# Stated load order and eight banks at the first MLP seam, and grad_out times gb made in the input-gradient loop

## The chip, the cores and the metric

One core of a Trainium2 chip runs the whole program. A core has five engines that run side by side and wait for each other through semaphores: TensorE (PE; its weight loads are shown as PEld), VectorE (DVE), ScalarE (ACT), GpSimd (POOL) and SyncE (SP). Here SP and POOL mainly issue DMA transfers, each from a list of its own that it works through from the top. The metric is the device time of one execution in microseconds (us); lower is better.

## The reference

A block with an adaptive layer norm, a spectral filter and an MLP, forward and backward, in bf16, with S = 2048 tokens, D = 1024 and F = 3584:

```python
mod = (silu(c) @ w_mod).reshape(1, 6, 1, -1)      # sa, ca, ga, sb, cb, gb
h = layernorm(x) * (1 + ca) + sa
x = x + ga * irfft2(rfft2(h) * (w_r + 1j * w_i))
h = layernorm(x) * (1 + cb) + sb
x = x + gb * (gelu(layernorm(h) @ w1 + b1) @ w2 + b2)
_out, _vjp = jax.vjp(f, x, w_r, w_i, w1, b1, w2, b2, c, w_mod)
return (_out, *_vjp(grad_out))
```

The outputs are the forward result and nine gradients. Three of the backward products matter here. The gradient of the MLP's input is gz @ w1^T, where gz (F x S) is the gradient before the gelu. The gradient of w2 is h^T @ (grad_out * gb). The gradient of row 5 of the modulation, gb, is the sum over the tokens of grad_out times the MLP's result.

## The kernel before

The tokens are worked in four blocks (b = 0 to 3) of 512, D in two halves (h) of 512, and F in seven groups (g) of 512. Buffers in on-chip memory are handed from one use to the next by tag: a tile that takes a tag over waits until the previous owner was read for the last time. PSUM has eight banks in three pools: ps_s with two, ps_d with two, ps_f with four. A scheduler orders the instructions of each engine and each DMA list when the kernel is built, by priority and by its own estimate of the time; `tc.issue_after(x)` keeps an instruction behind x in that order, and `ordered()` keeps the matmuls of the MLP in the order in which they are written.

**The MLP.** For each block and g, `z_block` (L781 to L817) makes the first product (pz, L795) and the gelu with its derivative, and stores hh and gz to DRAM. For each block and half, `bo_pass` (L822 to L860) makes the second product: a matmul with b2 (L827) opens four accumulators pbo, and then seven steps of 16 matmuls each (L836) read hh and one piece of w2. The pieces of w2 come through four buffers (w2sA, w2sC, w2sD, w2sB), 56 loads of 512 KB in all; each is issued by SP at L831, and the scheduler places it. At the end of a pass ScalarE copies pbo to otile (L845), VectorE makes the output from it, three stores write it to out_0 (one from SP, L154, and two from POOL, L159), and a later matmul pa (L855) sums the tokens of grad_out times the result, which VectorE adds into gacc. The plan at L872 to L878 interleaves z blocks and steps of bo_pass; block 3 has no z blocks beside it.

**The first MLP seam.** After the last pass come its pa, and pq (L903), which turns gacc into grad row 5 (`store_gmod`, L905: two casts at L177 and a store to d_gmod, L178), and ptr, which turns the gradient of b1 (L913). Then come the loads of the transposed w1 (L968 to L974): 28 DMA transposes of SP, four for each g, into tiles w1T that take over the tags of w1. The gradient loop reads gz from DRAM through eight slots (gzr, L1013).

**The input-gradient loop** (L1001 to L1054) runs for each block. TensorE makes pg, 2 halves x 7 g x 16 matmuls (L1020), in the four banks of ps_f, one half after the other. ScalarE copies pg to gn3 (L1025). VectorE and ScalarE take it backward through two layer norms: `ln_bwd` (L917 to L924) against n3u (loaded at L1005), the product with n2u into pru (L1032), again a scale (L1041) and `ln_bwd` against n2u, then the addition of grad_out (go4, which lies in got; loaded by `load_tok` at L1009, half of it by SP and half by two gathers of POOL, L130) at L1045. The sum is stored to d_gx1 (L1046). Its product with ga goes to n3u (L1048), is folded twice between n3u and pru (L1049) and lands in fbuf2 (L1050). Its product with d_A (au, L1047) is made at L1051. TensorE sums gn3 and pru over the tokens into acc3a (`sums3`, L1035), and au into acc3b (`sums3_ga`, L1053), which stands in the code after the block's work. Between these steps `early`, a ring of eight steps for grad row 5 (`gmod_ring`, L942 to L966), is advanced: each step is a product with a sum (L958), a scale (L960), a store to out_9 from POOL (L961) and the load of a later piece of w_mod by SP (L947); the ring starts when d_gmod has row 5 (L950).

**The seam to the gradient of w2.** After the loop, grad_out is loaded once more, a block at a time, with `load_tok`, into gB0 to gB3, which take over the tags of w1T tiles, and VectorE multiplies each by gb (L1059 to L1065). TensorE then makes gw2acc (L1114) from them and from transposed pieces of hh (hht, `hh_load` at L1139), and after 256 of these matmuls the backward spectral transform begins with pu (L470), which reads fbuf2.

Of the kernel before, what the change touches and what calls it, by code (L numbers as in the profile page):

```python
# [10 lines left out]
FP32 = mybir.dt.float32  # L11
BF16 = mybir.dt.bfloat16
# [5 lines left out]
P = 128  # L18
# [17 lines left out]
def kernel(  # L36
# [42 lines left out]
    def ps_f(name):  # L79
        return psum.tile([P, 512], FP32, tag="f", name=name, bufs=4)  # L80
# [38 lines left out]
    def chunk_rows(dt, i):  # L119
        return dt[4 * i * P:4 * (i + 1) * P, :].rearrange("(q p) d -> p q d", p=P)  # L120
# [4 lines left out]
    def load_tok(t4, src, i, eng=None):  # L125
        s3 = tok_flat(src)
        ins = (eng or nc.sync).dma_start(out=t4[:, 0:4:3, :],
                          in_=bass.AP(tensor=s3.tensor, offset=s3.offset + 128 * i * D, ap=[[D, P], [1024 * D, 2], [1, D]]))
        for q in range(2):
            nc.gpsimd.indirect_dma_start(out=t4[:, 1 + q, :], out_offset=None, in_=s3,  # L130
                                         in_offset=bass.IndirectOffsetOnAxis(ap=xidx[:, 2 * i + q:2 * i + q + 1], axis=0))
        return ins
# [687 lines left out]
    w2n = [0]  # L820

    def bo_pass(b, h):  # L822
        cs_ = slice(h * KH, (h + 1) * KH)
        pbs = [(ps_f if b < NB - 1 or h == 0 else (ps_s, ps_d)[k % 2])("pbo") for k in range(4)]
        for i in range(4):
            with ordered():
                last_pe[0] = nc.tensor.matmul(pbs[i][:], lhsT=ones_bf[0:1, :], rhs=b2_row[0:1, cs_], start=True, stop=False)  # L827
        for g in range(7):
            wp = w2p[w2n[0] % 4]
            w2n[0] += 1  # L830
            nc.sync.dma_start(out=wp, in_=w2_v[:, g * 4:(g + 1) * 4, cs_])  # L831
            hh = hh_slots[(b * 7 + g) % 11]
            for i in range(4):
                for k in range(4):
                    with ordered():
                        last_pe[0] = nc.tensor.matmul(pbs[i][:], lhsT=hh[:, k, i * P:(i + 1) * P], rhs=wp[:, k, :],  # L836
                                                      start=False, stop=(g == 6 and k == 3))
            if g < 6:
                yield
        bo, x1t, go = (otile[0][:, k] for k in range(3))  # L840
        nc.sync.dma_start(out=x1t, in_=chunk_rows(d_x1, b)[:, :, cs_])
        load_tok_half(go, grad_out, b, h)
        for i in range(4):
            with tc.high_priority():
                last_ev[0] = nc.scalar.copy(out=bo[:, i, :], in_=pbs[i][:])  # L845
        tt(go, go, bo, ALU.mult)
        tt(bo, bo, bcn(gb_row[:, cs_], 4), ALU.mult)
        tt(bo, bo, x1t, ALU.add)
        store_tok_half(out_0, bo, b, h)

        yield
        pa = (ps_d if b < NB - 1 else ps_f)("pa")
        for i in range(4):
            with ordered():
                last_pe[0] = nc.tensor.matmul(pa[32 * i:32 * (i + 1), :], lhsT=ones_bf[:, 0:32], rhs=go[:, i, :], start=True, stop=True)  # L855
# [24 lines left out]
    for kind, b, g in plan:  # L880
# [7 lines left out]
        else:  # L888
# [6 lines left out]
                bo_late.clear()  # L895
            if g == 13:
                next(boq[b], None)
    for late in bo_late:
        next(late, None)
    g5 = []  # L900
    for h in range(2):
        pq = (ps_s, ps_d)[h]("pq")
# [62 lines left out]
                load_w(n + 2)  # L965
            yield  # L966

    w1Ts = []  # L968
    for g in range(7):
        wtile = reg.tile([P, 4, D], BF16, name=f"w1T_{g}", tag=W1T[g])  # L970
        for k in range(4):
            fc = g * 4 + k
            nc.sync.dma_start_transpose(out=wtile[:, k, :], in_=B_w1[:, fc * P:(fc + 1) * P])
        w1Ts.append(wtile)  # L974
    gzr = [reg.tile([P, 2, 4, BW], BF16, name=f"gzr{k}", tag=f"t{k}") for k in range(4)]
    gn3s = [reg.tile([P, 4, D], BF16, name="gn3a", tag="uv0"), reg.tile([P, 4, D], BF16, name="gn3b", tag="wt")]
    n3u = reg.tile([P, 4, D], BF16, name="n3u", tag="uv1")
    n2u = reg.tile([P, 4, D], BF16, name="n2u", tag="uv2")
    pru = reg.tile([P, 4, D], BF16, name="pru", tag="uv3")[:]
# [3 lines left out]
    gzn = 0  # L983
# [14 lines left out]
    def sums3_ga(b, p4):  # L998
        halves_sum(acc3[1], p4, b == 0, b == 3)

    for b in range(NB):  # L1001
        gn3 = gn3s[b % 2]
        sums = small.tile([P, 2, 4], FP32, tag="sums")
        gzt = []
# [5 lines left out]
        for g in range(7):  # L1010
            sl = gzr[gzn % 8 // 2][:, gzn % 2]
            gzn += 1
            nc.sync.dma_start(out=sl, in_=d_gz_v[:, g * 4:(g + 1) * 4, b * BW:(b + 1) * BW])  # L1013
            gzt.append(sl)
        for h in range(2):
            pgs = [ps_f("pg") for _ in range(4)]
            for g in range(7):
                for i in range(4):
                    for k in range(4):
                        nc.tensor.matmul(pgs[i][:], lhsT=gzt[g][:, k, i * P:(i + 1) * P],  # L1020
                                         rhs=w1Ts[g][:, k, h * KH:(h + 1) * KH],
                                         start=(g == 0 and k == 0), stop=(g == 6 and k == 3))
            for i in range(4):
                with tc.high_priority():
                    nc.scalar.activation(out=gn3[:, i, h * KH:(h + 1) * KH], in_=pgs[i][:], func=ACT.Identity,  # L1025
                                         accum_out=sums[:, h, i:i + 1])
# [20 lines left out]
        nc.sync.dma_start(out=au[:], in_=chunk_rows(d_A, b))  # L1047
        tt(n3u[:], g2[:], bcn(ga_row, 4), ALU.mult)  # L1048
        fold_tok(n3u, ftmp)  # L1049
        fold2_in[b] = fold_d(fbuf2[:, b], n3u[:], ftmp)  # L1050
        tt(au[:], g2[:], au[:], ALU.mult)  # L1051
        if b < NB - 1:
            sums3_ga(b, au)  # L1053
            next(early, None)  # L1054


    hhp = reg.tile([P, 2, NT, P], BF16, name="hhsA", tag="px1")
    gBs = []
    for b in range(NB):  # L1059
        gb_t = reg.tile([P, 4, D], BF16, name=f"gB{b}", tag=PXT[2 + b])  # L1060
        gb_in = load_tok(gb_t, grad_out, b)
        with tc.high_priority():
# [218 lines left out]
```

## Time and profile before

| what | value |
|---|---|
| median of 3 runs | 1510.4 us (1502.69 to 1513.5) |
| the profiled execution | 1507.2 us, its span 1505.0 us |
| mean granted TensorE clock | 0.978 |
| TensorE, VectorE, ScalarE, GpSimd busy | 1408.0 (94%), 1068.8 (71%), 721.4 (48%), 371.6 us (25%) |
| moved by DMA | 324.27 MB, mean 215 GB/s |
| hardware queue (SP), software queue (POOL) | 51.3%, 22.5% of the 16 DMA engines' span |

The stages around the change, from the windows of the profile (the columns after the engine's name are its busy time and, in brackets, its instructions; then the granted clock, the DMA engines' busy share, and the rate):

```profile
core 0: us, PE busy (x) PEld busy (x) DVE busy (x) ACT busy (x) POOL busy (x), PEclk, DMA share, GB/s
...
720.00:740.00 20.00, 17.38 (x81) 7.64 (x82) 7.54 (x15) 0.00 (x0) 4.21 (x4) 1.00 1.08 366
...
760.00:780.00 20.00, 15.46 (x66) 6.37 (x67) 4.96 (x6) 6.56 (x8) 1.48 (x3) 0.93 0.55 187
...
880.00:940.00 60.00, 55.05 (x265) 24.42 (x268) 48.66 (x72) 23.07 (x34) 4.20 (x3) 1.00 0.45 158
...
990.00:1000.00 10.00, 0.84 (x3) 0.30 (x4) 2.29 (x1) 0.00 (x0) 2.47 (x1) 0.61 1.09 213
1000.00:1010.00 10.00, 6.18 (x17) 2.06 (x16) 6.16 (x8) 0.09 (x1) 0.00 (x0) 0.70 1.05 284
```

How to read a profile: a page gives each engine's busy time, then the chain of work that ended last, followed back from the end, with each engine's share of it. In a row of a timeline stand the start, the length, the engine, the line, the operation, what it writes and reads, how many instructions are merged in the row, and in brackets how long the engine sat idle before it and what ended that. Idle time of an engine costs something only if it delays the work that ends last.

### The profile page before, as it was taken

How to read it: one execution, taken by the hardware profiler on the slowest of the kernel's cores; microseconds unless marked ns; L12 is line 12 of the kernel's file. 1: busy time of each engine (PE TensorE's matmuls, PEld its weight loads, DVE VectorE, ACT ScalarE, POOL GpSimd, SP SyncE). 2: the span in 40 equal slices, each digit the busy share in tenths (PEclk: the TensorE clock that was granted, in tenths of full speed). 3: DMA queues.
4: the chain of work that ended last, by engine and by line, in shares of the span. 5: the costliest groups of instructions: out<-in, count | busy, mean ns of one | idle time of the engine just before them, and what ended most of it. 6: DMA issues, size and time to landing. Idle time of an engine off the chain costs nothing.

```text
span 1505.0 us, 18218 instructions
## 1 busy us (share of the span) xinstructions
PE 1408.0 (94%) x6703; PEld 655.0 (44%) x6835; DVE 1068.8 (71%) x1574; ACT 721.4 (48%) x960; POOL 371.6 (25%) x427
## 2 busy tenths in 40 slices
PE   5899989999999999999889999969999999899998
PEld 2434545444444444444334444424454444444443
DVE  5883777898799888877413877959067776997551
ACT  4765446757887755666111433313532344453211
POOL 5710631210112122212112001220124421222432
PEclk8999999999999999999999999989999999999999
DMA  9982664899687777899956246398379987675992
GB/s 336 265 223 67 156 212 137 264 245 338 225 252 230 233 243 231 247 279 262 344 195 221 76 180 224 107 214 211 98 188 241 248 221 222 175 198 149 275 294 92
DMA packets 358168, 324.27 MB, mean 215 GB/s; under 512 B 209191, under 2 KB 300861, under 8 KB 357824
## 3 DMA queue, kind: packets, MB, share of 16 engines
q1 hardware_dynamic: 324192, 207.71, 51.3%
q0 software_dynamic: 33888, 115.41, 22.5%
q8 instruction: 53, 0.87, 0.2%
q14 instruction: 35, 0.29, 0.1%
HBM read 164.15 MB, written 109.10 MB: 182 GB/s over the span
## 4 chain that ended last, share of the span: by engine, by line
PE 42%; DVE 19%; DMA 8%; issue 6%; ACT 5%; POOL 1%; SPq 0%; POOLq 0%; DVEq 0%; ACTq 0%
PE pbo L836 10%; PE pz L795 10%; PE gw2acc L1114 8%; PE gw1acc L1181 4%; PE pg L1020 4%; DVE ct L172 4%; DVE got L919 2%; PE pu L470 2%; PE pv L563 2%; ACT ct L460 1%; DVE gn3a L924 1%; DVE st L436 1%; DMA gB<-in_grad_out_dram 1%; DMA n3u<-d_n 1%; DMA w2sA<-in_B_w_dram 1%
## 5 line engine op out<-in xcount | busy, mean ns | idle before, releaser
L678 PE MATMUL pp<-gBoT,wt 128*128 128x512 bf16 x878 | 198.2, 383 | 4.9 <-DMA wt<-in_B_w_dram 2.0
L1020 PE MATMUL pg<-w1T,gzr 128*128 128x512 bf16 x876 | 195.2, 381 | 1.5 <-issue 0.7
L1181 PE MATMUL gw1acc<-gzh,n3n 128*128 128x512 bf16 x876 | 195.0, 381 | 1.1 <-issue 0.2
L678 PEld LDWEIGHTS <-wt 128*128 128x128 bf16 x896 | 88.0, 98 | 110.0 <-issue 6.1
L795 PEld LDWEIGHTS <-w 128*128 128x128 bf16 x896 | 87.5, 98 | 109.4 <-issue 6.0
L1020 PEld LDWEIGHTS <-gzr 128*128 128x128 bf16 x896 | 87.0, 98 | 108.5 <-issue 6.0
L1181 PEld LDWEIGHTS <-n3n 128*128 128x128 bf16 x896 | 87.6, 98 | 105.9 <-issue 2.4
L795 PE MATMUL pz<-n3Ta,w 128*128 128x512 bf16 x437 | 99.5, 383 | 2.9 <-ACT gt L798 2.1
L1114 PE MATMUL gw2acc<-gB,hhsA 128*128 128x512 bf16 x437 | 97.9, 379 | 1.0 <-DMA hhsA<-d_hh 0.4
L795 PE MATMUL pz<-n3Tb,w 128*128 128x512 bf16 x439 | 98.4, 379 | 0.5
L1119 ACT CAST gwo<-gw2acc 128x512 bf16<-128x512 f32 x54 | 30.5, 584 | 130.1 <-PE gw2acc L1114 84.1
L836 PEld LDWEIGHTS <-hhA 128*128 128x128 bf16 x608 | 58.9, 98 | 75.2 <-issue 5.1
L798 ACT ACTIVATE gt<-pz,b_col 128x512 bf16<-128x512 f32 x112 | 73.1, 683 | 35.6 <-PE pz L795 33.7
L1185 ACT CAST gwo<-gw1acc 128x512 bf16<-128x512 f32 x53 | 30.8, 582 | 115.1 <-PE gw1acc L1181 91.6
L804 ACT ACTIVATE gt<-gt 128x2048 bf16<-128x2048 bf16 x28 | 53.5, 1910 | 66.1 <-DVE gt L172 66.0
L172 DVE TENSOR_TENSOR gt<-gt,gt 128x2048 bf16<-128x2048 bf16 x56 | 68.5, 1223 | 21.6 <-ACT gt L806 20.9
L172 DVE TENSOR_TENSOR ct<-ct 128x2048 bf16<-128x2048 bf16 x64 | 75.9, 1221 | 10.3 <-ACT ct L631 9.0
L1114 PE MATMUL gw2acc<-gB,hht 128*128 128x512 bf16 x251 | 58.6, 393 | 14.4 <-DMA hht<-d_hh 10.3
L1114 PEld LDWEIGHTS <-hhsA 128*128 128x128 bf16 x448 | 43.6, 98 | 52.5 <-DMA hhsA<-d_hh 0.9
L800 ACT ACTIVATE gt<-gt 128x2048 bf16<-128x2048 bf16 x28 | 53.4, 1907 | 0.6
L806 ACT ACTIVATE gt<-gt 128x2048 bf16<-128x2048 bf16 x28 | 53.4, 1907 | 0.5
L1186 POOL DMA_DIRECT2D out_dram<-gwo x56 | 30.5, 546 | 84.5 <-ACT gwo L1185 74.3
(313 smaller groups left out, 2495.2 us busy)
## 6 DMA issues: line engine op xcount, KB each, us to landing
gzr<-d_gz SPq DMA_DIRECT2D x28, 512.0 KB, 6.4
wblk<-in_w_mod_dram SPq DMA_DIRECT2D x12, 1024.0 KB, 9.7
d_ph<-pho POOLq DMA_DIRECT2D x21, 512.0 KB, 5.6
out_dram<-otl POOLq DMA_DIRECT2D x40, 256.0 KB, 3.6
d_hh<-hhA POOLq DMA_DIRECT2D x19, 512.0 KB, 4.8
w2sD<-in_B_w_dram SPq DMA_DIRECT2D x14, 512.0 KB
hhC<-d_ph SPq DMA_DIRECT2D x14, 512.0 KB, 4.9
w2sA<-d_ph SPq DMA_DIRECT2D x14, 512.0 KB, 4.5
```

The source lines that it names most:

```text
L172: return nc.vector.tensor_tensor(out=out, in0=a, in1=b, op=op)
L678: last_pe[0] = nc.tensor.matmul(pp[:], lhsT=wt[:, fg % 2, cch, k * P:(k + 1) * P], rhs=gBoT[j][:, cch, :], start=(cch == 0), stop=(cch == ...
L795: last_pe[0] = nc.tensor.matmul(pz[:], lhsT=w1s[g][:, cch, k * P:(k + 1) * P], rhs=n3T[:, cch, :], start=(cch == 0), stop=(cch == NDC - 1))
L798: nc.scalar.activation(out=zb[:, k, :], in_=pz[:], func=ACT.Identity, bias=b1_col[:, fc:fc + 1], scale=1.0)
L800: nc.scalar.activation(out=av, in_=zb, func=ACT.Square)
L804: nc.scalar.activation(out=sg, in_=bv, func=ACT.Sigmoid, scale=2.0 * GK)
L806: nc.scalar.activation(out=bv, in_=bv, func=ACT.Sigmoid, scale=-2.0 * GK)
L836: last_pe[0] = nc.tensor.matmul(pbs[i][:], lhsT=hh[:, k, i * P:(i + 1) * P], rhs=wp[:, k, :], start=False, stop=(g == 6 and k == 3))
L1020: nc.tensor.matmul(pgs[i][:], lhsT=gzt[g][:, k, i * P:(i + 1) * P], rhs=w1Ts[g][:, k, h * KH:(h + 1) * KH], start=(g == 0 and k == 0), sto ...
L1114: nc.tensor.matmul(acc[:], lhsT=hh_s[hh_o[fc]][:, t, :], rhs=gBs[t // 4][:, t % 4, h * KH:(h + 1) * KH], start=(t == 0), stop=(t == NT - 1))
L1181: nc.tensor.matmul(acc[:], lhsT=n3ns[t // 4][:, t % 4, cch * P:(cch + 1) * P], rhs=gz2[t // 8][:, t % 8, :], start=(t == 0), stop=(t == NT ...
L1185: nc.any.tensor_copy(out=ob, in_=acc[:])
```

## The change

Two edits, made together. In the first, the loads at the first MLP seam have a stated order. `w2_load` issues the w2 pieces and keeps them in a list; in block 3 a piece is asked for three steps ahead. Transposes of w1T from the ninth on are put behind the w2 loads of block 3, one behind each, and the gz loads of block 0 behind the 12th, 13th and 14th of them. `pg_pass` makes pg step by step. For block 0 both halves run in turn, half 0 in the four banks of ps_f and half 1 in those of ps_s and ps_d, so that all eight hold accumulators; the order of halves is 0, 0, 1, 0, 1, and so on. The first two steps stand before the last pa. pa of block 3, half 0 uses a bank of ps_f, and the others ps_d. pq and ptr come after block 0's pg. gn3 takes other tags (uv3 and wt; pru takes uv0). sums3_ga of a block moves behind the next block's pg.

In the second, the product of grad_out and gb is made in the loop from go4, which is there anyway. For blocks 0 to 2 it is stored to a new DRAM tensor d_gB and loaded back in one piece each by SP, into the same gB tiles; for block 3 it goes straight to the tile. The four reloads by load_tok and the four products behind the loop are gone.

```diff
+    d_gB = dram.tile([3 * BW, D], BF16, name="d_gB")
...
+    w2_in = []
+    def w2_load(upto):
+        while len(w2_in) <= min(upto, NB * 14 - 1):
+            n = len(w2_in)
+            h, g = n // 7 % 2, n % 7
+            w2_in.append(nc.sync.dma_start(out=w2p[n % 4], in_=w2_v[:, g * 4:(g + 1) * 4, h * KH:(h + 1) * KH]))
...
-            wp = w2p[w2n[0] % 4]
-            w2n[0] += 1
-            nc.sync.dma_start(out=wp, in_=w2_v[:, g * 4:(g + 1) * 4, cs_])
+            n = (2 * b + h) * 7 + g
+            w2_load(n + 3 if b == NB - 1 else n)
+            wp = w2p[n % 4]
...
-        pa = (ps_d if b < NB - 1 else ps_f)("pa")
+        pa = (ps_f if (b, h) == (NB - 1, 0) else ps_d)("pa")
...
+    def behind_w2(k):
+        return tc.issue_after(w2_in[(NB - 1) * 14 + min(max(k, 0), 13)].ins)
+    for g in range(7):
+        wtile = reg.tile([P, 4, D], BF16, name=f"w1T_{g}", tag=W1T[g])
+        for k in range(4):
+            fc = g * 4 + k
+            with behind_w2(fc - 8) if fc >= 8 else ExitStack():
+                nc.sync.dma_start_transpose(out=wtile[:, k, :], in_=B_w1[:, fc * P:(fc + 1) * P])
+        w1Ts.append(wtile)
+        with behind_w2(11 + g):
+            load_gz(0, g)
...
+    pg0 = [pg_pass(0, 0, lambda k: ps_f, ordered), pg_pass(0, 1, lambda k: (ps_s, ps_d)[k // 2], ordered)]
+    for n, h in enumerate((0, 0, 1, 0, 1, 0, 1, 0, 1, 0, 1, 0, 1, 1)):
+        if n == 2:
+            for late in bo_late:
+                next(late, None)
+        next(pg0[h])
...
+        if b > 0:
+            for g in range(7):
+                load_gz(b, g)
+            for h in range(2):
+                for _ in pg_pass(b, h, lambda k: ps_f):
+                    pass
+            with tc.issue_after(last_pg[0].ins):
+                sums3_ga(b - 1, au)
+        gn3 = gn3_of(b)
+        if b == NB - 1:
+            gb3 = reg.tile([P, 4, D], BF16, name="gB3", tag="px5")
+            tt(gb3[:], go4, bcn(gb_row, 4), ALU.mult)
...
         nc.gpsimd.dma_start(out=chunk_rows(d_gx1, b), in_=g2[:])
+        if b < NB - 1:
+            tt(go4, go4, bcn(gb_row, 4), ALU.mult)
+            nc.gpsimd.dma_start(out=chunk_rows(d_gB, b), in_=go4)
...
-            sums3_ga(b, au)
...
-    for b in range(NB):
+    for b in range(NB - 1):
         gb_t = reg.tile([P, 4, D], BF16, name=f"gB{b}", tag=PXT[2 + b])
-        gb_in = load_tok(gb_t, grad_out, b)
-        with tc.high_priority():
-            with tc.issue_after(fold2_in[2].ins):
-                tt(gb_t[:], gb_t[:], bcn(gb_row, 4), ALU.mult)
+        gb_in = nc.sync.dma_start(out=gb_t[:], in_=chunk_rows(d_gB, b))
         gBs.append(gb_t)
+    gBs.append(gb3)
```

More of the change, by code (lines that the diff above doesn't have):

```diff
@@ L819 @@
     w2_v = B_w2.rearrange("(c p) d -> p c d", p=P)
-    w2n = [0]
+    w2_in = []
[4 more added lines that the diff above has]
+            w2_in.append(nc.sync.dma_start(out=w2p[n % 4], in_=w2_v[:, g * 4:(g + 1) * 4, h * KH:(h + 1) * KH]))
     def bo_pass(b, h):
@@ L897, with gn3_of, load_gz @@
                 next(boq[b], None)
-    for late in bo_late:
-        next(late, None)
+    w1Ts = []
+    gzr = [reg.tile([P, 2, 4, BW], BF16, name=f"gzr{k}", tag=f"t{k}") for k in range(4)]
+    gzs, g_sums, gn3s = {}, {}, {}
+    def gn3_of(b):
+        if b % 2 not in gn3s:
+            gn3s[b % 2] = reg.tile([P, 4, D], BF16, name=f"gn3{'ab'[b % 2]}", tag=("uv3", "wt")[b % 2])
+        return gn3s[b % 2]
+    def load_gz(b, g):
+        n = b * 7 + g
+        gzs[b, g] = gzr[n % 8 // 2][:, n % 2]
+        nc.sync.dma_start(out=gzs[b, g], in_=d_gz_v[:, g * 4:(g + 1) * 4, b * BW:(b + 1) * BW])
@@ new lines, with pg_pass @@
+    last_pg = [None]
+    def pg_pass(b, h, pool, before=lambda: ExitStack()):
+        pgs = [pool(k)("pg") for k in range(4)]
+        for g in range(7):
+            for i in range(4):
+                for k in range(4):
+                    with before():
+                        last_pg[0] = nc.tensor.matmul(pgs[i][:], lhsT=gzs[b, g][:, k, i * P:(i + 1) * P],
+                                                      rhs=w1Ts[g][:, k, h * KH:(h + 1) * KH],
+                                                      start=(g == 0 and k == 0), stop=(g == 6 and k == 3))
+                    last_pe[0] = last_pg[0]
+            if g < 6:
+                yield
+        for i in range(4):
+            with tc.high_priority():
+                nc.scalar.activation(out=gn3_of(b)[:, i, h * KH:(h + 1) * KH], in_=pgs[i][:], func=ACT.Identity,
+                                     accum_out=g_sums[b][:, h, i:i + 1])
+        yield
@@ L900 @@
+    g_sums[0] = small.tile([P, 2, 4], FP32, name="sums", tag="sums")
+    pg0 = [pg_pass(0, 0, lambda k: ps_f, ordered), pg_pass(0, 1, lambda k: (ps_s, ps_d)[k // 2], ordered)]
[4 more added lines that the diff above has]
+        next(pg0[h])
     g5 = []
@@ L966, in gmod_ring @@
             yield
[L968 to L976, printed above, removed]
     n3u = reg.tile([P, 4, D], BF16, name="n3u", tag="uv1")
     n2u = reg.tile([P, 4, D], BF16, name="n2u", tag="uv2")
-    pru = reg.tile([P, 4, D], BF16, name="pru", tag="uv3")[:]
+    pru = reg.tile([P, 4, D], BF16, name="pru", tag="uv0")[:]
     got = reg.tile([P, 6, D], BF16, name="got", tag="ot")
@@ L982 @@
     acc3 = [ps_d("acc3a"), ps_d("acc3b")]
-    gzn = 0
     gmw = reg.tile([P, 2, D], BF16, name="gmw", tag="ph")
@@ L1001 @@
     for b in range(NB):
-        gn3 = gn3s[b % 2]
-        sums = small.tile([P, 2, 4], FP32, tag="sums")
-        gzt = []
+        if b > 0:
+            g_sums[b] = small.tile([P, 2, 4], FP32, name="sums", tag="sums")
+        sums = g_sums[b]
         nc.sync.dma_start(out=n3u[:], in_=chunk_rows(d_n3, b))
@@ L1009 @@
         load_tok(go4, grad_out, b)
[L1010 to L1016, printed above, removed]
-            for g in range(7):
[L1018 to L1023, printed above, removed]
-                with tc.high_priority():
-                    nc.scalar.activation(out=gn3[:, i, h * KH:(h + 1) * KH], in_=pgs[i][:], func=ACT.Identity,
-                                         accum_out=sums[:, h, i:i + 1])
+        if b > 0:
+            for g in range(7):
+                load_gz(b, g)
[8 more added lines that the diff above has]
+            tt(gb3[:], go4, bcn(gb_row, 4), ALU.mult)
         tt(sums[:, 0, :], sums[:, 0, :], sums[:, 1, :], ALU.add)
@@ L1058 @@
     gBs = []
-    for b in range(NB):
+    for b in range(NB - 1):
         gb_t = reg.tile([P, 4, D], BF16, name=f"gB{b}", tag=PXT[2 + b])
-        gb_in = load_tok(gb_t, grad_out, b)
-        with tc.high_priority():
-            with tc.issue_after(fold2_in[2].ins):
-                tt(gb_t[:], gb_t[:], bcn(gb_row, 4), ALU.mult)
+        gb_in = nc.sync.dma_start(out=gb_t[:], in_=chunk_rows(d_gB, b))
         gBs.append(gb_t)
+    gBs.append(gb3)
     smA2 = reg.tile([P, 2, 4, 512], BF16, name="smA2", tag="sma")
```

## The prediction

> **What bounds the kernel now.** I read the page first, then TensorE's timeline around both places that the diff names, then VectorE's and SP's timelines of the loop between them. The page:
>
> ```profile
> PE 42%; DVE 19%; DMA 8%; issue 6%; ACT 5%; POOL 1%; SPq 0%; POOLq 0%; DVEq 0%; ACTq 0%
> ```
>
> TensorE is busy 94% of the span, so only its waits can be won. On TensorE's timeline (start, length, instruction, in brackets the idle time before it and what ended it), first the seam from the second MLP product (pbo) to the gradient loop (pg), then the loop, then the seam to the weight gradient:
>
> ```profile
> 716.19 0.86 PE L827 MATMUL pbo<-b_row,ones_bf 1*128 1x512 bf16 x2 [1.85 <-ACT otile L845]
> 726.16 3.61 PE L836 MATMUL pbo<-w2sA,hhB 128*128 128x512 bf16 x15 [1.76 <-DMA w2sA<-in_B_w_dram]
> 733.98 3.61 PE L836 MATMUL pbo<-w2sD,hhA 128*128 128x512 bf16 x16 [0.76 <-DMA w2sD<-in_B_w_dram]
> 773.16 1.02 PE L903 MATMUL pq<-w2sD,quad 128*1 128x512 f32 x2 [1.51 <-ACT otile L845]
> 777.00 0.42 PE L855 MATMUL pa<-otile,ones_bf 128*32 128x512 bf16 x4 [2.65 <-DVE otile L172]
> ```
> ```profile
> 886.33 0.39 PE L195 MATMUL acc3a<-gn3b,ones_bf 128*32 128x512 bf16 x2 [1.73 <-DVE gn3b L924]
> 999.16 3.55 PE L1114 MATMUL gw2acc<-gB,hht 128*128 128x512 bf16 x8 [10.27 <-DMA hht<-d_hh]
> 1006.18 1.87 PE L1114 MATMUL gw2acc<-gB,hht 128*128 128x512 bf16 x4 [3.48 <-DVE gB L172]
> ```
>
> Inside the loop TensorE waits little, yet it waits for VectorE (886.33), and VectorE's own timeline shows why:
>
> ```profile
> 826.71 1.23 DVE L919 CUSTOM_DVE_ANT_0 got<-gn3a,n3u 128x1024 bf16<-128x1024 bf16 x1 [10.23 <-ACT gn3a L1025]
> 872.79 2.36 DVE L172 TENSOR_TENSOR fbuf<-pru 128x2048 bf16<-128x2048 bf16 x2
> 880.74 1.23 DVE L919 CUSTOM_DVE_ANT_0 got<-gn3b,n3u 128x1024 bf16<-128x1024 bf16 x1 [5.59 <-DMA n3u<-d_n]
> ```
>
> n3u has one buffer. VectorE reads it last at 872.78, SP issues the next load at 872.78, and the next block's work starts at 880.74. So the loop is a chain of 46.1 us VectorE plus 8.0 us load per block: starts at 826.71, 880.74, 934.71 (54.0 apart), while TensorE needs some 50. This chain decides what reaches the end.
>
> **The change, part by part.** Sums are against the profiled execution: 1507.2 us, span 1505.0 and 2.2 around it; the median of the runs, 1510.4, is 3.2 above it.
>
> First seam. From 713.74 to the end of pg of block 0 (828.55) 114.8 us pass. The work in it: 448 large matmuls at 0.216 (16 start 3.45 apart), two bias rows of 0.97, three pa of 0.33, two pq of 0.97, ptr 0.2: 101.9. So 12.9 are lost, 9.9 in idle rows (the five above, and 0.72, 0.27 and 0.33), the rest in matmuls of double length after them. In the built order of the changed kernel SP has at most one or two w1T transposes between two w2 loads, where it had four (10.36 us of SP's time at 697.18). Each w2 load then issues when its buffer comes free, some 10 us ahead of its use, against 4.4 us to landing: its waits go. The two waits at 773 and 777 go under the 32 pg matmuls put there (6.9 us). The late w1T and gz meet no new wait: both halves together use one g in 6.9 us, the last tiles are needed some 38 us into pg, and 9 transposes at 2.5 us and 7 gz loads fit. The 1.85 stays. pq and ptr (2.1) move behind pg. So VectorE's block 0 starts 12.9 - 1.85 + 2.1 = 13.2 earlier. From that I take 1.0, because SP's out store of the next-to-last pass still stands before a w2 load: -12.2, start 814.5. If the loads fail altogether, 3.5 of it is lost.
>
> Block 0 of the chain. The eight early steps for grad row 5 (L958, L960) ran from 791 to 817, when VectorE had nothing else. They need pq, and pq now comes after pg. In the built order, five L958 (1.15 from start to start), four L960 (0.40), the new product with gb (2.25), and two L177 and one L188 (1.5) stand before the last read of n3u: 11.1. They fill idle rows of 1.11, 1.06 and 1.37 there: +7.6, so n3u is free at 53.7 after the start. But its load waits longer. SP has before it the load of got, which waits until the d_gB store has landed, and a gmw load, which waits for an out_9 store; on POOL that store is queued behind the two got gathers, which wait for d_gB as well. No trace shows a d_gB store; d_gx (L1046), equal in bytes and queue, is the nearest row:
>
> ```profile
> DMA to landing us min/median/max: 7.4/8.8/11.5
> ```
>
> At 8.8: d_gB issues at 40.6 and lands at 49.4, gathers 3.8 (1.59, 0.30, 1.89), out_9 store 0.5 + 3.3, n3u issued at 57.0, next start at 65.0 instead of 54.0: +11.0 (bounds +7.6, where the store costs nothing, and +14).
>
> The Trainium skill, page "SBUF — State Buffer", section "Who interferes with whom", says that tensor_scalar in a two-port mode shuts GpSimd out for its whole length, so that descriptors of its queue come late. By that rule two L960 beside d_gB would make it +11.8; no run here shows it.
>
> Block 1: the product, 2.25, and one more early step, 1.55, of which about 1.0 fills an idle row: +2.8. Its got load (store landed 47.2) stands before n3u (free at 48.9) without holding it. Were the store 20 us, as the gB gathers at most took, it would.
>
> Block 2 and the second seam. Before, 73.6 us lie between the starts of blocks 2 and 3 (934.71 and 1008.32), because VectorE did the four gB products first (2.29 each) and waited for their loads between them. These go: three blocks come back from d_gB as whole loads, the fourth is made from got. Eight POOL gathers (12.2 us median to landing) go too. In their place SP has, before n3u: got (after d_gB), gB2, and a transpose of hht. SP issues its list in order, and a transpose can hold it:
>
> ```profile
> 970.19 14.48 SPq L1139 DMA_TRANSPOSE hht<-d_hh  x1
> 984.77 0.52 SPq L1047 DMA_DIRECT2D au<-d_A  x1
> ```
>
> I take d_gB landed 46 to 48 after the start, 0.9 for two issues, 6 for the transpose (20.43 for three behind it, 14.48 at worst), 8.0 for n3u: 62 instead of 73.6, -11.6 (bounds 56.4, from block 1's chain, and 72).
>
> To the end. Before, the first pu matmul came 54.3 after block 3's start. Now TensorE is at its sums early: pg of block 3 ends 48.7 after block 2's start, 96 gw2acc take 20.7, and the pru that acc3a sums is ready only 15.7 after block 3's start, so it waits some 8 us there. After that come 1.0 of sums and 160 x 0.216 = 34.6, and slow matmuls: eight took 3.55 after the 10.27 wait, 1.8 too much. 15.7 + 1.0 + 34.6 + 1.8 = 53.1: -1.2. fbuf is ready at 45.8 and hides.
>
> The waits at 999 and 1006 thus do not simply vanish; they are paid in the chain. New waits of some 8 and 5 us stand at the acc3a of blocks 1 and 2 and cost nothing more. From pu on nothing is moved except one eviction. Moving sums3_ga behind pg removes three waits of 1.1 on TensorE, which has slack: 0.
>
> Sum: -12.2 + 11.0 + 2.8 - 11.6 - 1.2 = **-11.2**: profiled 1496, median 1499.
>
> **The rivals.**
> - Faster: the chain is not held by the stores. For it: d_gx landed in 7.4 at best, the out_9 steps may be early, and the transpose can issue quickly (2.0 at least). Against: three waits in line. Block 0 at +7.6 and block 2 at 58 give -12.2 + 7.6 + 2.8 - 15.6 - 1.2 = -18.6: 1492.
> - Slower: the d_gB store. If it lands 20 us after its issue instead of 8.8, got holds SP's queue and n3u behind it: +11 in block 0, +9.5 in block 1 (1.7 slack), +11 in block 2, together +31.5 and a result of +20: 1531. It decides against the change from about 13 us on. For it: the gB gathers in the same queue took up to 20.3. Against: those met a transpose and 6 MB of other loads, while this store meets 3 MB at blocks 0 and 1.
> - The seam does not do what it says: single transposes of 2.5 us and the out store still make w2 late, or w1T is late for pg. Then 3.5 to 7 of the 12.2 stay: 1504.
>
> **How the numbers follow.** Chances: forecast 0.50 (1493 to 1506), faster rival 0.26, seam rival 0.14, store rival 0.10. The range reaches from 1486 (the faster rival with the shortest transpose and the full 13.2, 1490, less 4 for the spread of the median, whose runs lie 3 to 8 from it) to 1516 (the forecast's 1506 with one store landing 10 us late), which leaves out most of the store rival and the end of the faster one. A measurement of this kernel can tell about 1% (15 us) from no change. Faster by over 1%, below 1495.3: most of the faster rival and a fifth of the forecast, 0.33. Slower by over 1%, above 1525.5: half of the store rival and a little, 0.06. Within: 0.61.
>
> **What would show it.** Right: no DMA wait in pbo after 720; block 0's L919 at about 814; L958 rows between L1041 and the folds of block 0; n3u's second issue some 57 us after that start, just after an out_9 store; TensorE idle 5 to 9 us at the first acc3a of blocks 1 and 2; pu at about 1051. Wrong, if the block starts stand 54 apart, if n3u issues as soon as it is read, or if TensorE's largest wait is still for hht.

## The result, and the profile after

The changed kernel takes 1515.3 us (median of 22 runs, 1511.8 to 1521.1), the kernel before 1510.4 in the same comparison (22 runs, 1501.7 to 1517.0): a ratio of 1.0044, 95% interval 1.0030 to 1.0058. The profiled execution has a span of 1512.5 us against 1505.0, so 7.5 longer, and 11.2 shorter was forecast. The rows of this section are from the changed kernel's profile, where nothing else is said.

TensorE's timeline at the first seam (start, length, instruction, in brackets the idle time before it and what ended it):

```profile
716.01 0.86 PE L834 MATMUL pbo<-b_row,ones_bf 1*128 1x512 bf16 x2 [1.85 <-ACT otile L852]
724.15 3.63 PE L843 MATMUL pbo<-w2sA,hhB 128*128 128x512 bf16 x15
767.11 7.07 PE L940 MATMUL pg<-w1T,gzr 128*128 128x512 bf16 x31
774.11 0.40 PE L862 MATMUL pa<-otile,ones_bf 128*32 128x512 bf16 x4
```

The waits for w2 are gone, pa comes after the first pg steps without a wait, and pg begins at 767.11 instead of 777.76. VectorE's timeline has the starts of the four blocks, and what stands before the fourth:

```profile
814.22 1.23 DVE L978 CUSTOM_DVE_ANT_0 got<-gn3a,n3u 128x1024 bf16<-128x1024 bf16 x1 [38.97 <-ACT gn3a L948]
880.97 1.23 DVE L978 CUSTOM_DVE_ANT_0 got<-gn3b,n3u 128x1024 bf16<-128x1024 bf16 x1 [3.68 <-DMA n3u<-d_n]
939.27 1.23 DVE L978 CUSTOM_DVE_ANT_0 got<-gn3a,n3u 128x1024 bf16<-128x1024 bf16 x1 [7.07 <-DMA n3u<-d_n]
...
1011.19 2.29 DVE L173 TENSOR_TENSOR gB<-got,rows 128x4096 bf16<-128x4096 bf16 x1 [23.83 <-DMA got<-in_grad_out_dram,xu]
1013.40 2.35 DVE L173 TENSOR_TENSOR fbuf<-pru 128x2048 bf16<-128x2048 bf16 x2
...
1015.99 1.22 DVE L978 CUSTOM_DVE_ANT_0 got<-gn3b,n3u 128x1024 bf16<-128x1024 bf16 x1
```

Before, they were 826.71, 880.74, 934.71 and 1008.32; the last start and the first pu of that profile:

```profile
1008.32 1.22 DVE L919 CUSTOM_DVE_ANT_0 got<-gn3b,n3u 128x1024 bf16<-128x1024 bf16 x1
...
1062.59 13.98 PE L470 MATMUL pu<-smA,fbuf 128*128 128x512 bf16 x63
```

The gain of 12.5 at the first start is gone at the second, and at the fourth the kernel is 7.7 late. VectorE's longest wait inside the loop, 23.83, stands before the product gB3, and behind it in VectorE's list wait the last folds of block 2 and all of block 3. TensorE waits for the same:

```profile
886.12 0.61 PE L196 MATMUL acc3a<-gn3b,ones_bf 128*32 128x512 bf16 x2 [10.36 <-DVE gn3b L983]
944.42 0.61 PE L196 MATMUL acc3a<-gn3a,ones_bf 128*32 128x512 bf16 x2 [6.24 <-DVE gn3a L983]
...
997.85 3.59 PE L1158 MATMUL gw2acc<-gB,hht 128*128 128x512 bf16 x8 [8.72 <-DMA hht<-d_hh]
1006.38 1.86 PE L1158 MATMUL gw2acc<-gB,hht 128*128 128x512 bf16 x4 [4.94 <-DMA gB<-d_gB]
1013.53 20.97 PE L1158 MATMUL gw2acc<-gB,hht 128*128 128x512 bf16 x82 [5.29 <-DVE gB L173]
...
1069.95 13.98 PE L471 MATMUL pu<-smA,fbuf 128*128 128x512 bf16 x62
```

pu begins at 1069.95 instead of 1062.59, 7.4 later; from there to the end both take about the same, 442.6 and 442.4. GpSimd's timeline shows why got was late: the gathers of the next block wait in its list for the d_gB store.

```profile
854.20 0.76 POOL L1093 DMA_DIRECT2D d_gB<-got  x1 [2.32 <-DVE got L173]
863.18 2.10 POOL L131 DMA_INDIRECT got<-in_grad_out_dram,xu  x1 [8.22 <-DMA d_gB<-got]
...
918.25 0.76 POOL L1093 DMA_DIRECT2D d_gB<-got  x1 [1.30 <-DVE got L173]
928.32 2.00 POOL L131 DMA_INDIRECT got<-in_grad_out_dram,xu  x1 [9.31 <-DMA d_gB<-got]
...
976.19 0.80 POOL L1093 DMA_DIRECT2D d_gB<-got  x1 [1.28 <-DVE got L173]
998.76 1.03 POOL L131 DMA_INDIRECT got<-in_grad_out_dram,xu  x1 [21.77 <-DMA d_gB<-got]
```

The same megabyte needs about 9, 10 and 22 us from issue to landing. In the third case a transpose of hht was issued 4.4 us ahead of it. SP's list at that place:

```profile
971.75 12.62 SPq L1183 DMA_TRANSPOSE hht<-d_hh  x1
998.03 0.38 SPq L128 DMA_DIRECT2D got<-in_grad_out_dram  x1
998.51 0.42 SPq L1107 DMA_DIRECT2D gB<-d_gB  x1
998.98 7.25 SPq L1183 DMA_TRANSPOSE hht<-d_hh  x1
1006.33 0.53 SPq L1054 DMA_DIRECT2D n3u<-d_n  x1
```

SP stands still from 984.4 to 998.0 for the store, with gB2, the next transpose and n3u of block 3 behind. On the page, the chain that ended last has the store in it (2% by line), and TensorE's share of the chain grows from 42% to 45%.

### The profile page after: what moved, and what is told of

The parts are those of the page before. It is cut to its first block, busy times and chain, and to the rows that moved or that the text cites. A ratio compares the mean times of both kernels' runs of the same rounds, so it can differ in the third digit from the quotient of the medians.

```text
span 1512.5 us, 18196 instructions
## 1 busy us (share of the span) xinstructions
PE 1406.6 (93%) x6703; PEld 655.1 (43%) x6835; DVE 1068.4 (71%) x1575; ACT 722.2 (48%) x959; POOL 361.9 (24%) x422
## 4 chain that ended last, share of the span: by engine, by line
PE 45%; DVE 16%; DMA 9%; issue 7%; ACT 4%; POOL 1%; SPq 1%; POOLq 0%; DVEq 0%; ACTq 0%
PE pbo L843 12%; PE pz L796 10%; PE gw2acc L1158 6%; PE pg L940 6%; PE gw1acc L1225 5%; DVE ct L173 4%; DMA d_gB<-got 2%; PE pu L471 2%; DVE got L978 1%; DMA n3u<-d_n 1%; ACT ct L461 1%; PE pp L679 1%; DVE gt L173 1%; DVE ct L1141 1%; DVE ct L978 1%
## 5 line engine op out<-in xcount | busy, mean ns | idle before, releaser
L805 ACT ACTIVATE gt<-gt 128x2048 bf16<-128x2048 bf16 x28 | 53.5, 1910 | 67.1 <-DVE gt L173 67.1
```

Source lines behind the costliest of these rows:

```text
L805: nc.scalar.activation(out=sg, in_=bv, func=ACT.Sigmoid, scale=2.0 * GK)
```

## The experiments

All ratios are to the kernel before, measured beside each run. "Block lengths" are the distances between the first layer-norm rows of successive blocks on VectorE, in each kernel's own profile; for comparison:

| kernel | first start | block 0 | block 1 | block 2 | to pu | span |
|---|---|---|---|---|---|---|
| before | 826.7 | 54.0 | 54.0 | 73.6 | 54.3 | 1505.0 |
| forecast | 814.5 | 65.0 | 56.8 | 62 | 53.1 | 1494 |
| after | 814.2 | 66.8 | 58.3 | 76.7 | 54.0 | 1512.5 |
| first edit alone | 819.3 | 59.9 | 55.1 | 67.9 | 55.2 | 1501.6 |
| second edit alone | 825.1 | 56.5 | 57.8 | 67.6 | 53.7 | 1505.0 |

**Each edit by itself.** The first kernel has the loads, the eight banks and the late pq, and the loop and the reload of before:

```diff
-            tt(go4, go4, bcn(gb_row, 4), ALU.mult)
-            nc.gpsimd.dma_start(out=chunk_rows(d_gB, b), in_=go4)
...
+        gb_in = load_tok(gb_t, grad_out, b)
+                tt(gb_t[:], gb_t[:], bcn(gb_row, 4), ALU.mult)
```

> The first edit alone (order of the loads, eight banks), with the reload of grad_out and its four products behind the loop as before. Theory A, that both edits push cost into VectorE's chain: block 0 starts at about 814 (before 826.7), the eight steps for grad row 5 fall into the loop and make block 0 about 62 us long instead of 54 (no store of the product to wait for), blocks 1 and 2 stay at about 55 and 73.6. The span is then 4 to 5 us shorter than before, a ratio of 0.997. Theory B, that the second edit alone carries the loss: block 0 stays at 54 and the span is 12 us shorter, 0.992. Theory C, that the first edit is itself a loss: ratio above 1.000.

Measured: 0.9972 (0.9945 to 1.0000), the ratio of theory A, though not by its parts. Block 0 is 5.8 longer than before though it has no d_gB store: that is the price of the steps for grad row 5 inside the loop, seven of them in block 0 and one in block 1. With it the seam's gain is used up, since block 2 starts at 934.2 and before at 934.7. What is left is block 2, 67.9 where theory A had 73.6; why it is shorter was not sought. Block 0 starts at 819.3, not 814.2, with the same code up to there. The difference is on TensorE: it is 2.1 late already at 718, and there 16 matmuls take 6.31 us instead of 3.63, after the same wait of 1.85; from 719 to 722 the granted clock is 0.50 here and 1.00 in the changed kernel. In the seven profiles with this seam and pq behind pg the start lies between 814.2 and 819.3, with a mean of 817.0.

The second kernel has the product and d_gB on the seam of before:

> The second edit alone (the product made in the loop, three blocks through d_gB), on the kernel before. The steps for grad row 5 run ahead of block 0 as before. Theory A: block 0 takes 57 to 60 us instead of 54 (2.3 for the product, the rest for the load of got that waits for the store and stands before n3u's), block 1 the same, and block 2 about 76 instead of 73.6, since the store of block 2 lands some 20 us after its issue; the span is 8 to 14 us longer, a ratio of 1.005 to 1.010. Theory B, that the long store of block 2 came only from how the first edit had shifted the work: block 2 takes 62, and the span is 4 to 8 us shorter, 0.995 to 0.997.

Measured: 0.9998 (0.9971 to 1.0025), in neither theory's range. Blocks 0 and 1 are 2.5 and 3.8 longer, about as theory A said. Block 2 is 67.6, between the two theories: its store landed 18.0 us after its issue (977.59 to 995.57, again beside a transpose), but no transpose stands between gB2 and n3u here. So neither edit alone costs what the two cost together: 1501.6 and 1505.0, and with both 1512.5.

**The transposes beside the store.** The first four transposes of hht are put behind n3u of block 3:

```diff
-            hh_in[0] = nc.sync.dma_start_transpose(out=hh_s[hh_o[fc]], in_=d_hh[fc * P:(fc + 1) * P, :])
+            with tc.issue_after(n3u_in.ins) if fc < 4 else ExitStack():
+                hh_in[0] = nc.sync.dma_start_transpose(out=hh_s[hh_o[fc]], in_=d_hh[fc * P:(fc + 1) * P, :])
```

> The changed kernel with the first four transposes of hht placed in SP's list behind the load of n3u for block 3. Theory A, that the transposes slow the d_gB store of block 2 and hold the list: the store lands 9 to 12 us after its issue instead of 21.7, the load of got issues at about 987 instead of 998, the product gB3 ends at about 998 instead of 1013.4, block 3 starts at about 999 instead of 1016, pu comes at 1055 to 1060 instead of 1070 (the first hht is then late itself), and the ratio to the kernel before is 0.992 to 0.997. Theory S, that the store is slow by itself in that place (behind d_gx in the same queue): it still lands 18 us or more after its issue, and the time is within 3 us of the changed kernel, 1.002 to 1.006.

GpSimd's and VectorE's timelines of this run:

```profile
978.03 0.80 POOL L1093 DMA_DIRECT2D d_gB<-got  x1 [1.28 <-DVE got L173]
987.35 1.62 POOL L131 DMA_INDIRECT got<-in_grad_out_dram,xu  x1 [8.52 <-DMA d_gB<-got]
```
```profile
996.69 2.29 DVE L173 TENSOR_TENSOR gB<-got,rows 128x4096 bf16<-128x4096 bf16 x1 [7.49 <-DMA got<-in_grad_out_dram,xu]
...
1001.49 1.21 DVE L978 CUSTOM_DVE_ANT_0 got<-gn3b,n3u 128x1024 bf16<-128x1024 bf16 x1
```

The store lands about 9 us after its issue, and block 3 starts 14.5 earlier than in the changed kernel: theory A's cause is right. The DMA counts of the two kernels (packets, MB and share of each queue), first the changed one while the store and the transpose are both under way (980 to 996), then this one without a transpose (978.5 to 987: stores, and 0.46 MB of loads) and with transposes alone (1003.5 to 1008):

```profile
DMA packets 2114, 2.32 MB, mean 145 GB/s; under 512 B 1649, under 2 KB 1649, under 8 KB 2113
q1 hardware_dynamic: 1619, 0.41, 67.2%
q0 software_dynamic: 494, 1.90, 42.2%
```
```profile
DMA packets 785, 2.57 MB, mean 303 GB/s; under 512 B 48, under 2 KB 48, under 8 KB 784
q0 software_dynamic: 544, 2.10, 60.7%
q1 hardware_dynamic: 240, 0.46, 16.1%
...
DMA packets 3883, 0.99 MB, mean 219 GB/s; under 512 B 3883, under 2 KB 3883, under 8 KB 3883
```

In the mixed stretch both queues together move 145 GB/s. At the rates of the other two, its 1.90 MB of stores and 0.41 MB of transposes would take 6.3 + 1.9 = 8.2 us; they took 16. But the time was missed: 1.0030 (1.0001 to 1.0059), where 0.992 to 0.997 was expected. The transposes are needed too. gw2acc cannot start before 1004.10 now, the scheduler put six pu matmuls ahead of it, which wait 4.84 for their own operand and 3.36 for the folds behind gB3, and pu goes on at 1064. What the store won, the late transposes took.

**n3u ahead of everything.** SP's list for block 3 in another order, with gB3 behind the first layer norm, and a constraint on TensorE that keeps pu behind gw2acc:

```diff
+        with tc.issue_after(n3u_in.ins) if b == NB - 1 else ExitStack():
+            go_in = load_tok(go4, grad_out, b)
...
+        with tc.issue_after(go_in.ins) if b == 2 else ExitStack():
             gb_in = nc.sync.dma_start(out=gb_t[:], in_=chunk_rows(d_gB, b))
...
+            with tc.issue_after(go_in.ins) if 1 <= fc < 4 else ExitStack():
```

> The changed kernel with SP's list for block 3 in another order: n3u first, then got, and gB2 and the transposes of hht from the second on behind them; the product gB3 comes after the first layer norm of block 3. Theory D, that the chain over block 3's start sets the end: n3u is issued at about 988 instead of 1006, block 3 starts at about 997 instead of 1016, and pu follows 54 us later, at about 1052, a ratio of 0.99. Theory T, that TensorE is late by itself, since it gets gB2 and gB3 only after the store of block 2 has landed: block 3 starts at 997 too, but gB3 is not done before some 1009, and the 240 matmuls that still follow it put pu at 1064 to 1068; the ratio is 1.000 to 1.004.

```profile
1014.77 0.61 PE L196 MATMUL acc3a<-gn3b,ones_bf 128*32 128x512 bf16 x2 [8.73 <-DVE gn3b L985]
```

Measured: 1.0029 (1.0001 to 1.0057), pu at 1069.4. n3u was issued at 992.4, 14 us earlier than in the changed kernel, but its load, in the same stretch as the store and the transpose, landed only at 1008.4, 16 us later (8.0 before). Block 3 starts at 1008.45, 7.5 earlier than in the changed kernel, and pu follows 61.0 later, not 54 as theory D has it: the ratio and the 1069.4 are nearer to theory T. Yet TensorE's last wait before pu, to 1014.77, is for block 3's first layer norm, and gB3 is done at 1013.5, so the two reach the end almost together and the run doesn't tell them apart. It does show that a plain load beside the store and the transpose was slow too.

**Only the second to the fourth transpose later.** The same edit as in the run with the transposes beside the store, with `1 <= fc < 4`: the first transpose still meets the store.

> The changed kernel with only the second to the fourth transpose of hht behind the load of n3u for block 3; the first stays where it is, beside the d_gB store of block 2. Theory T, that the late landing of that store (got, gB2 and the product gB3 behind it) sets the end through TensorE: the store still lands 18 us or more after its issue, block 3 starts some 5 us earlier (1008 to 1011 instead of 1016), but gB3 is done at 1009 to 1012 as before and pu comes at 1066 to 1069; ratio 1.001 to 1.004. Theory L, that the transpose between gB2 and n3u in SP's list is what costs: pu follows block 3's start by 54 us, at 1062 or earlier, and the ratio is 0.995 to 0.999.

```profile
1011.09 2.29 DVE L173 TENSOR_TENSOR gB<-got,rows 128x4096 bf16<-128x4096 bf16 x1 [19.47 <-DMA got<-in_grad_out_dram,xu]
...
1015.89 1.22 DVE L978 CUSTOM_DVE_ANT_0 got<-gn3b,n3u 128x1024 bf16<-128x1024 bf16 x1
```

Measured: 1.0029 (1.0001 to 1.0057), with the store landing 20.5 us after its issue, gB3 at 1011 to 1013.4 and pu at 1069.5 (three of its matmuls run at 1019), about as theory T said. n3u was issued 4 us earlier, and block 3 starts at 1015.9 as in the changed kernel, and not at 1008 to 1011, because gB3 stands ahead of it in VectorE's list. Block 2 starts 3.8 later in this profile, so it is 72.8 long instead of 76.7: the transpose between gB2 and n3u costs some 4 us at most, and the late got is the rest.

**pq back ahead of pg.** Halves in the order 0, 0, pa, 0, 0, pq, 0, 1, 1, 1, 1, 0, 1, 0, 1, 1, and got of block 0 behind the load of d_gmod:

```diff
-    for n, h in enumerate((0, 0, 1, 0, 1, 0, 1, 0, 1, 0, 1, 0, 1, 1)):
+    for n, h in enumerate((0, 0, 0, 0, 0, 1, 1, 1, 1, 0, 1, 0, 1, 1)):
...
+        if n == 4:
+            for hq in range(2):
+                pq = (ps_s, ps_d)[hq]("pq")
...
+            store_gmod(g5, 5)
```

> The changed kernel with pq put back ahead of most of block 0's pg: the halves run in the order 0, 0, pa, 0, 0, pq, 0, 1, 1, 1, 1, 0, 1, 0, 1, 1, and the load of got for block 0 stands behind that of d_gmod, so that the eight steps for grad row 5 can run while VectorE waits for pg. Theory A, that the steps inside the loop (and the out_9 stores and gmw loads that come with them) cost block 0 some 10 us: block 0 starts at 815 to 818, takes 56 to 58 us instead of 66.8, blocks 1 and 2 stay at 58 and 73 to 77, and the ratio to the kernel before is 0.996 to 0.999 (the changed kernel: 1.004). Theory S, that the d_gB store alone makes block 0 long: it stays above 62, and the ratio is above 1.001.

Measured: 0.9952 (0.9924 to 0.9980), a little better than theory A had. Block 0 takes 58.2 us instead of 66.8: theory A. It starts at 824.3, however, and not at 815 to 818, since all eight steps stand before it on VectorE and their buffers come round only at 824. Block 2 took 66.1, where 73 to 77 was expected; the store landed 14.4 us after its issue.

The same without the second edit:

> The first edit alone, with pq early, and the reload of grad_out and its four products behind the loop as before. If the steps for grad row 5 are all that took the first edit's gain away, block 0 starts at 815 to 818 and takes 54 us, blocks 1 and 2 about 55 and 68, pu comes at 1047 to 1051, and the ratio is 0.989 to 0.992; against the first edit alone (0.997) that is the price of putting pq behind pg. If TensorE's start of the second seam or the reload sets the end, block 2 grows by what the others win and the ratio stays at 0.996 or more.

Measured: 0.9940 (0.9915 to 0.9964), between the two expected ranges, pu at 1051.4. Block 0 is 52.4 long, so the steps were its whole excess; but it starts at 822.7 for the same reason as above, and block 2 grows to 71.0, with TensorE waiting 10.08 for the product of a reloaded piece. TensorE's last long wait is then for the reload; whether the second edit is worth having beside this seam, with its store out of the way, the runs of both repairs below tell.

**The product early.** VectorE is idle at the start of each block, and pru is free there. The product goes into it, and got is never held:

```diff
+        else:
+            tt(pru, go4, bcn(gb_row, 4), ALU.mult)
+            nc.gpsimd.dma_start(out=chunk_rows(d_gB, b), in_=pru)
...
-        if b < NB - 1:
-            tt(go4, go4, bcn(gb_row, 4), ALU.mult)
-            nc.gpsimd.dma_start(out=chunk_rows(d_gB, b), in_=go4)
```

The first of these runs also has the second to the fourth transpose behind n3u of block 3:

> The changed kernel with the product by gb of blocks 0 to 2 made at the start of the block, where VectorE waits for n3u, into pru (which is free until the first product with n2u) and stored from there, so that got is not held by the store; and the transposes of hht from the second to the fourth behind the load of n3u for block 3. The steps for grad row 5 stay in the loop. Theory A, that the place of the store is what made the edit a loss: block 0 takes about 60 us instead of 66.8, block 1 about 55 instead of 58.3, block 2 57 to 62 instead of 76.7; TensorE then sets the end, pu comes at 1047 to 1052 instead of 1070, a ratio of 0.990 to 0.993. Theory H, that the transposes of hht and the traffic of the second seam set it anyhow: block 2 stays above 68, and the ratio is 0.996 or more.

Measured: 0.9847 (0.9791 to 0.9903), pu at 1042.6; block lengths 59.3, 54.4 and 59.4. The lengths are those of theory A, and the time is better than it had. Without the order for the transposes:

> The kernel with the early product into pru, without the order for the transposes of hht. Theory A, that the place of the product and of its store did all of it: block 2 takes 59 to 62 us and the ratio is 0.983 to 0.988, as with the order. Theory L, that the order was needed too: a second transpose stands before n3u in SP's list, n3u is issued some 8 us later, block 2 takes 67 to 70 us, and the ratio is 0.989 to 0.993.

Measured: 0.9873 (0.9821 to 0.9926), pu at 1042.4; block lengths 59.3, 54.5 and 60.7. So the order does next to nothing, and theory A holds: the place of the product and of its store did it. Against the changed kernel pu comes 27.5 earlier: block 0 gives 7.4 of it, block 1 3.8, block 2 16.0 and the stretch to pu 2.4, while the first start is 2.1 later. GpSimd's and VectorE's timelines of the second run:

```profile
928.20 0.80 POOL L1073 DMA_DIRECT2D d_gB<-pru  x1 [11.22 <-DVE pru L173]
965.50 0.80 POOL L1093 DMA_DIRECT2D d_gx<-gn3a  x1 [36.50 <-issue]
966.60 1.59 POOL L131 DMA_INDIRECT got<-in_grad_out_dram,xu  x1 [0.30 <-DMA n2u<-d_x]
```
```profile
977.21 2.29 DVE L173 TENSOR_TENSOR gB<-got,rows 128x4096 bf16<-128x4096 bf16 x1 [3.06 <-DMA got<-in_grad_out_dram,xu]
990.82 1.22 DVE L978 CUSTOM_DVE_ANT_0 got<-gn3b,n3u 128x1024 bf16<-128x1024 bf16 x1 [6.66 <-DMA n3u<-d_n]
```

The store of block 2 is issued at 928, long before the transposes, the gathers follow d_gx at once, and gB3 is done at 979.5 instead of 1013.5.

**Both repairs.** pq early, six of the eight steps ahead of block 0 and two between blocks 0 and 1, the product early, and the second to the fourth transpose behind n3u:

> Both repairs together: pq early as in the kernel with pq put back, with six of the eight steps for grad row 5 ahead of block 0 and two between blocks 0 and 1, and the product made early into pru. Theory A: blocks of 54 to 55, 54 to 55 and 57 to 62 us from a start at 815 to 818, pu at 1038 to 1046, a ratio of 0.984 to 0.988. Theory H, that the second seam is bound by the transposes of hht and other traffic: no more than 3 us better than the kernel with the early product alone.

Measured: 0.9820 (0.9765 to 0.9876), block lengths 53.8, 51.7 and 57.8, pu at 1034.1: better than theory A had, and by the medians 4.7 us better than the early product alone. Against the same seam with the reload, 0.9940 (0.9915 to 0.9964), the second edit is now a gain (two steps and three transposes are moved as well). Once more, for a narrower interval:

> The kernel with both repairs once more, in more rounds, for a narrower interval: 0.980 to 0.985 of the kernel before if the first measurement holds.

Measured: 0.9813 (0.9772 to 0.9854), median 1480.6 us against 1507.9 before. Of TensorE's waits at both seams and in the loop there remain these over 0.6 us:

```profile
716.07 0.86 PE L834 MATMUL pbo<-b_row,ones_bf 1*128 1x512 bf16 x2 [1.86 <-ACT otile L852]
...
875.36 0.39 PE L196 MATMUL acc3a<-gn3b,ones_bf 128*32 128x512 bf16 x2 [2.10 <-DVE gn3b L984]
927.41 0.39 PE L196 MATMUL acc3a<-gn3a,ones_bf 128*32 128x512 bf16 x2 [0.66 <-DVE gn3a L984]
```

This version is faster than both kernels, by 27 us than the one before.

## Why the prediction was right and wrong

The sum was -11.2 and the span grew by 7.5: the direction was wrong. The median, 1515.3, lies just below the range's upper end of 1516, which had been set for one store that lands 10 us late, and inside the 1% around the kernel before. One store did land late, by 13 us, and blocks 0 and 1 were longer than forecast too, so that the median is still inside the range owes something to luck. Term by term, in us:

| step | forecast | measured |
|---|---|---|
| first seam | -12.2 | -12.5 |
| block 0 | +11.0 | +12.7 |
| block 1 | +2.8 | +4.3 |
| block 2 and second seam | -11.6 | +3.1 |
| to the end | -1.2 | -0.3 |

**First seam: right in mechanism, and the size is one profile's.** No wait for w2 after 720, block 0 at 814.2 against "about 814". Over the seven profiles with this seam the mean start is 817.0, and in the two with the seam of before 826.7 and 825.1: the seam is worth about 9. In one of the seven (n3u ahead of everything) TensorE still waits 2.08 for a piece of w2, at 742.35.

**Block 0: right, somewhat small.** The steps for grad row 5 do fill the loop; d_gB was issued at 40.0 and landed at 48.8 after the start (forecast 40.6 and 49.4), the gathers took 4.4 (3.8), the out_9 store and the gmw load behind them held n3u until 59.2 (57.0). In this profile n3u was free at about 866.7, 52.4 after the start, and was issued at 873.45, behind that gmw load (872.21). The runs bear out that the two edits work together here. In the four kernels with this seam n3u is issued 46.6 us after the start with neither the steps nor the product in the loop (pq early, first edit alone), 52.2 with the steps, 48.8 with the product and its store, and 59.2 with both: the steps make 5.6, the product 2.2 and the two together 12.6, since the out_9 store stands behind gathers that wait for d_gB. The lengths of block 0 alone (52.4, 59.9, 58.2 and 66.8) don't show it, because the load of n3u took 5.8, 7.7, 9.5 and 7.5 us in them. The Trainium skill, page "SBUF — State Buffer", section "Who interferes with whom", has tensor_scalar in a two-port mode hold GpSimd up for its whole length. No run here can tell: one such scale (L1019, at 860.50, 0.48 us) fell beside the store, which landed 8.8 us after its issue (854.20 to 862.97), and without one, in the run of the second edit alone, it landed after 8.7 (862.20 to 870.92).

**Block 1: right, 1.5 small.** The store landed 47.1 after the start (forecast 47.2) and n3u was issued at 48.7 (48.9); its load took 9.6 us instead of 8.0.

**Block 2: this is the step that failed.** "I take d_gB landed 46 to 48 after the start", and from there to "62 instead of 73.6". The store was issued where it should be, 36.9 after the start, and landed at 58.8, so that the block took 76.7: 14.7 of the 18.7 us between forecast and measurement are here. The 46 to 48 took the 8.8 us of d_gx for the landing, a median over four blocks. The rows before said otherwise for this place. The d_gx of block 2, issued at 969.95 with a transpose right behind it in SP's list (970.19), was the one of 11.5, and the gB gathers from 974.8 to 983.1 took 15.7 to 20.3 (the view of line L1046 from 960 to 1010 in the kernel before):

```profile
L1046 POOL DMA_DIRECT2D d_gx<-gn3a x1: 800/800/800, 969.9 to 969.9; - x1
DMA to landing us min/median/max: 11.5/11.5/11.5
```

The median of the eight gB gathers was 17.8; the 12.2 in the prediction mixes in the gathers of got. The prediction had the rule for it: the slower rival said that gathers of this queue had taken 20.3 us beside a transpose, and answered that the store "meets 3 MB at blocks 0 and 1". That holds for blocks 0 and 1 alone. At block 2 the store meets a transpose, which the prediction itself placed in SP's list at that very spot. The run with all four transposes behind n3u takes them away and finds 9 us. So the rival came true in one block of three, beyond its point of decision (13 us). The second half of the error is VectorE's list: the forecast let block 3 start when n3u had landed, but gB3 stands ahead of it and needs got, hence the store, the load and two gathers. The run with only the later transposes moved bears this out: n3u was issued 59.4 after the start of block 2 instead of 67.1, and block 3 still started only when gB3 and the folds were done.

**To the end: the size came out by luck, for another reason.** Forecast was a wait of some 8 us at the acc3a of block 3, with pru late. There is none. TensorE gets gB3 at 1013.5 and then works 56.4 us without a pause to pu, of which 244 matmuls at 0.216 make up 52.7. It came to acc3a at 1034.4, when pru had been ready since 1031.8: TensorE's own backlog was the later of the two by 2.6 us.

**The waits at acc3a** of blocks 1 and 2 were forecast at 5 to 9 us and measured at 10.4 and 6.2; they cost nothing more, as was said. **"TensorE's largest wait is still for hht"** was named as a sign of being wrong. At the second seam it was that, 8.72; the largest of all was the 10.36 at acc3a. pu was to come at about 1051 and came at 1069.95.

## What to carry to other kernels

A store that is put on the path because its buffer is reloaded should be timed against what is in the DMA queues at each place where it occurs, not against a median: one of three met a transpose and took twice as long. A product needs its place chosen as much as its operands: moved from the busy end of a block to an idle stretch with a free buffer, the same product and the same store went from a loss of 0.4% to a gain of 1.3% (interval 0.7% to 1.8%). And where an in-order list holds the start of the next stage, look for every instruction in front of it, on VectorE as on SP.

## What was not expected of the hardware

A DMA transpose and stores from the software queue together moved far less than either by itself: 145 GB/s, against 219 for transposes alone and 303 for stores and a few loads without one. The Trainium skill, page "Advanced Engine Details and Errata", section "X-Bar Transpose (TRN2)", calls transposes as fast as regular transfers. The trace does not agree for this shape: 219 against 303. That the small packets of the transpose (under 512 B) are what slows the mixture was not tried by itself. The landing of the block 2 store beside the transpose varied: 14.4, 18.0, 19.3, 20.5 and 21.8 us in five kernels.

After a wait of TensorE of the same length, 1.85, the next 16 matmuls took 3.63 us in the changed kernel and 6.31 in the first experiment, in code that is the same. The granted clock from 719 to 722 was 1.00 in the one and 0.50 in the other. What decided that is not shown; a few microseconds between single profiles say nothing about the code.
